# Which engine squares the score tiles of batch 1: GpSimd from the third batch's bursts on only

## The chip, the cores and the metric

One Trainium2 chip, one of its cores. A core has five engines, each with its own queue of instructions that it works through in order: TensorE (PE in the profile; its weight loads are listed apart as PEld), VectorE (DVE), ScalarE (ACT), GpSimd (POOL) and SyncE (SP), which here only issues DMAs. Matmul results go to PSUM, which GpSimd does not read in this kernel; everything else lies in SBUF. The metric is the device time of one execution in microseconds (us); lower is better.

## The reference

Attention with a squared ReLU in place of the softmax, and behind it a feed-forward block whose activation is a squared ReLU too. Cut to what is computed:

```python
# q, k, v: 8 batches, 12 heads, 448 tokens, 64 wide (float32)
scores = scale * np.matmul(q, k.transpose(0, 1, 3, 2))     # scale = 1/8
attn = np.maximum(scores, 0.0) ** 2 / S                    # S = 448
attn_out = np.matmul(attn, v)
x = attn_out.transpose(0, 2, 1, 3).reshape(B * S, H * D)   # 3584 x 768
h = x @ w_in                                               # 768 x 2048
r = np.maximum(h, 0.0)
out = (r * r) @ w_out                                      # 2048 x 768
```

## The kernel before

**Units, rounds, bursts.** Four heads of one batch are a unit `n`; three units make a batch, 24 in all. A unit has seven rounds `t`, each of 64 keys. A round makes one score tile `sp` (eight small matmuls per pair of rounds, L384), squares its positive part into an fp16 tile `at` (`soft`), and later multiplies `at` with v (`av`, L416). The first 23 rounds (batch 0 and two rounds more) are one stream. From there on the rounds go in pairs: burst `i` does rounds `2i` and `2i + 1`, for `i` from 11 to 83 (burst 11 has one round only). Within a burst TensorE first makes the score tiles, then, in the bursts that `avs` names, all seven products of a finished unit (28 matmuls), and then as much of the feed-forward block as `run_some` takes from a queue of pieces of work.

**What fills the bursts.** That queue (`push_dense`) holds for each batch 16 h groups (six matmuls each, L198, with the squared ReLU of h behind them) and the products with w_out. Batch 0 uses plain products (16 matmuls, L236); later batches use a form with fewer products (`o_groups`), which needs sums and differences of blocks of w_out, eight in all, made once by `combine_w2` on GpSimd (L145 to L151) and set between the h groups of batch 0. In bursts 11 to 18 TensorE does two h groups a burst, in bursts 19, 20 and 22 the four plain products.

**Two ways to square a tile.** `relu2` (L179): ScalarE squares the score tile into `at`, and VectorE multiplies `at` with a mask of the positive scores, reading the tile again. `relu2_wide` (L184): ScalarE writes the ReLU in fp32 to a buffer `rel`, of which there are two, and the engine that is named squares it into `at`. Score tiles lie in two PSUM buffers of two banks; the matmul results of all other work rotate through four more banks. The choice is made in `soft` (L390): from burst 12 on the first tile of a burst goes by `relu2`, the second, by `pool=z == 1` (L528), by `relu2_wide` with GpSimd.

**What sets the order.** TensorE and SP run in the order in which the program is written. The order on VectorE, ScalarE and GpSimd is set by the scheduler that builds the program. GpSimd has, beside the squares, the loads of v and of the weights (it issues their DMAs), the casts of k and q to fp16 (L96), the sums of w_out and a copy `rest` (L219). SP has the loads of k and q (L87), their transposes by DMA for units from 6 on (L102), and the stores of the output (L209). `upkeep` names the burst in which each of these is issued.

```python
    NU, TJ = 3, 7                       # units of a batch, rounds of a unit
    def av_burst(n):                    # the burst in which unit n's products run
        return (TJ * (n + 1) - 1) // 2 + 2
```

So the products of units 3, 4, 5 and 6 run in bursts 15, 19, 22 and 26, and `av_burst(2 * NU - 1)`, which the change uses, is 22.

Of the kernel before, what the change touches and what calls it, by code (L numbers as in the profile page):

```python
# [16 lines left out]
def kernel(  # L17
# [20 lines left out]
    NU = 3  # L38
# [131 lines left out]
    def run_some(ns):  # L170
        nonlocal queued, credit
        credit += ns
        while fifo and credit > 0:
            c, fn = fifo.popleft()
            fn()
            queued -= c
            credit -= c

    def relu2(ps, dst, scale):  # L179
        nc.scalar.activation(out=dst, in_=ps, func=AF.Square, scale=scale)  # L180
        nc.vector.scalar_tensor_tensor(  # L181
            out=dst, in0=ps, scalar=0.0, in1=dst, op0=ALU.is_gt, op1=ALU.mult)

    def relu2_wide(ps, dst, scale, eng):  # L184

        r = rel_p.tile([P, 2, S], FP32, name="rel", tag="wide")
        nc.scalar.activation(out=r, in_=ps, func=AF.Relu, scale=scale)  # L187
        eng.tensor_mul(dst, r, r)  # L188
# [149 lines left out]
    def push_dense(b):  # L338

        hs = h_groups(b)  # L340
        if b == 0:
            new = [[g] for c in range(2) for g in plain_groups(chunk(b, c))]
        elif b % 2 == 0:
            new = chain([o_groups(chunk(b, 0), chunk(b, 1))])
        else:
            pr = b // 2
            pairs = [o_groups(chunk(b - 1, 2), chunk(b, 0)), o_groups(chunk(b, 1), chunk(b, 2))]
            if pr % 2 == 1:
                pairs.insert(1, o_groups(rest_chunk(pr - 1), rest_chunk(pr)))
            new = chain(pairs)  # L350
        old = backlog[:QUOTA[b]]
        done = 0
        for i, g in enumerate(hs):
            push([g])
            upto = (i + 1) * len(old) // len(hs)
            for z in old[done:upto]:
                push(z)
            done = upto
            if b == 0 and 4 <= i < 16 and i % 2 == 1:
                push([(0.0, lambda k=(i - 4) // 2: combine_w2(k, nc.gpsimd))])  # L360
        if b % 2 == 1:
            push([(0.0, lambda: rest(b // 2))])
        backlog[:] = backlog[len(old):] + new
        now = QUOTA[b] - len(old)
        for z in backlog[:now]:
            push(z)
        del backlog[:now]
        if b == 0:
            push([(0.0, lambda k=k: combine_w2(k, nc.gpsimd)) for k in (6, 7)])
# [7 lines left out]
    def scores(n, t):  # L377
        qT, kT = qkt[n, "q"], qkt[n, "k"]
        sp = s_p.tile([P, 2, 512], FP32, name="sp", tag="s")
        for e in range(2):  # L380
            for f in range(2):
                c = f ^ e
                r = slice(64 * f, 64 * f + 64)
                nc.tensor.matmul(  # L384
                    sp[64 * c:64 * c + 64, e, 0:S].rearrange("p (t c) -> p t c", t=TJ),
                    lhsT=kT[r, t, 64 * e:64 * e + 64],
                    rhs=qT[r, :, 64 * e:64 * e + 64], start=True, stop=True)
        return sp

    def soft(n, t, sp, pool=False):  # L390
        at = at_p.tile([P, 2, S], FP16, name="at", tag="at")
        if pool:
            relu2_wide(sp[:, :, 0:S], at, SK, nc.gpsimd)
        elif n < NU and t % 2 == 1:
            relu2_wide(sp[:, :, 0:S], at, SK, nc.gpsimd if n == 1 and t == 3 else nc.vector)
        else:
            relu2(sp[:, :, 0:S], at, SK)
        ats[n, t] = at
# [3 lines left out]
    def av(n, t):  # L402

        b, u = divmod(n, NU)
        if n == NU * b and t == 0:
            xts[b] = x_p.tile([P, NM, S], FP16, name="xt", tag="xt")
        vs = vst[n]
        if t == 0:
            avs_open[n] = [mm_p.tile([P, 512], FP32, name="avt", tag="mm") for _ in range(2)]
        ap = avs_open[n]  # L410
        at = ats.pop((n, t))
        for e in range(2):
            for c in range(2):
                f = c ^ e
                r = slice(64 * c, 64 * c + 64)
                nc.tensor.matmul(  # L416
                    ap[f][64 * e:64 * e + 64, 0:S],
                    lhsT=vs[r, e ^ c, t * D:(t + 1) * D],
                    rhs=at[r, e, :],
                    start=(t == 0), stop=(t == TJ - 1), skip_group_check=True)  # L420
        if t < TJ - 1:
            return
        for f in range(2):
            nc.scalar.activation(  # L424
                out=xts[b][:, 2 * u + f, :], in_=ap[f][:, 0:S], func=AF.Copy, scale=CX)

    pool, dve, act = nc.gpsimd.tensor_copy, nc.vector.tensor_copy, nc.scalar.copy
# [9 lines left out]
    def av_burst(n):  # L437
        return (TJ * (n + 1) - 1) // 2 + 2
# [4 lines left out]
    def upkeep(i):  # L443

        for n in range(NU, NUN):
            b, u = divmod(n, NU)
            if i == av_burst(n - 1) and NU + 2 < n + 3 < NUN:
                load_v(n + 3)
            if i == max(TJ * n // 2, STREAM // 2):
                if 5 < n + 3 < NUN:  # L450
                    for w in "kq":
                        load_qk(n + 3, w, nc.sync)
            if i == (TJ * n + 4) // 2:
                if n + 2 < NUN:
                    for w in "kq":
                        cast_qk(n + 2, w, pool)
                if n + 1 < NPE:
                    turn_pe(n + 1, "k", dve)
                    turn_pe(n + 1, "q", act)
                if NPE <= n + 2 < NUN:  # L460
                    for w in "kq":
                        turn_dma(n + 2, w)
# [56 lines left out]
    for i in range(STREAM // 2, NB):  # L519
        g = []  # L520
        for r in range(max(STREAM, 2 * i), 2 * i + 2):
            n, t = divmod(r, TJ)
            g.append((n, t, scores(n, t)))
        if i in avs:
            for t in range(TJ):
                av(avs[i], t)
        for z, a in enumerate(g):
            soft(*a, pool=z == 1)  # L528
        if i in pushes:
            push_dense(pushes[i])  # L530
        upkeep(i)
        nxt = min([j for j in pushes if j > i] or [NB + 2])
        run_some(max(0.0, (queued - KEEP) / (nxt - i)))
# [37 lines left out]
```

## Time and profile before

| | |
|---|---|
| time, median of 2 runs | 424.2 us (424.13 to 424.28) |
| profiled execution, its own time | 422.38 us |
| span of that execution, first to last instruction | 420.6 us |
| mean granted clock of TensorE | 0.963 |
| busy: TensorE, VectorE, ScalarE, GpSimd | 378.7, 259.4, 259.3, 234.9 us |
| squares by GpSimd (L188), number and mean | 73, 1687 ns |
| Relu into `rel` (L187, ScalarE), mean | 922 ns |
| Square into `at` (L180, ScalarE), mean | 915 ns |
| mask of a score tile (L181, VectorE), mean | 1088 ns |

The profiled execution is one run with a hardware profile. Its span leaves out what lies ahead of the first and behind the last instruction, 1.8 us here. A row of a timeline has the start and duration in us, the engine, the line, the operation, what is written and what is read (tile names without buffer numbers), the shape and a count; the bracket at its end holds the time for which the engine had stood idle, and what ended that.

### The profile page before, as it was taken

Reading aid. Unit: us, or ns where it says so; the run is one execution under the profiler, and the core shown is the slowest. Engines: PE = TensorE matmul, PEld = TensorE weight load, DVE = VectorE, ACT = ScalarE, POOL = GpSimd, SP = SyncE. Lnnn points to the kernel's source line nnn. Section 1 sums busy time; section 2 is a strip of 40 time slices with the busy share of each in tenths; the row PEclk is TensorE's granted clock in tenths of the full one; section 3 lists DMA queues with packets and bytes.
Section 4 is the critical chain, followed back from the end, with each engine's and each line's share of the span. In section 5 each row is a group of like instructions: output and inputs, shape, how many; then the busy total and the mean of one; then the engine's idle time right before and its main releaser. Section 6 shows DMA issues by size and latency. Waiting matters only on the chain.

```text
span 420.6 us, 7636 instructions
## 1 busy us (share of the span) xinstructions
PE 378.7 (90%) x3000; PEld 190.2 (45%) x3000; DVE 259.4 (62%) x336; ACT 259.3 (62%) x407; POOL 234.9 (56%) x197
## 2 busy tenths in 40 slices
PE   6847736989999999999999999998998999999995
PEld 2424312444444544444455545544444444555562
DVE  3978521733669367857798655874696566545831
ACT  3888523875876587768856677676765767234111
POOL 6761889989965664865866645736753433200000
PEclk9698955999999999999999999999999999999999
DMA  8999994346715977369247674483633201120243
GB/s 255 295 257 234 238 199 110 67 104 149 218 22 89 216 161 147 68 166 245 60 83 189 169 184 73 145 179 61 170 41 80 59 2 39 37 58 0 51 101 75
DMA packets 67620, 53.58 MB, mean 127 GB/s; under 512 B 36865, under 2 KB 67585, under 8 KB 67585
## 3 DMA queue, kind: packets, MB, share of 16 engines
q1 hardware_dynamic: 55152, 40.84, 38.2%
q0 software_dynamic: 12160, 11.80, 18.4%
q8 instruction: 23, 0.38, 0.4%
q10 hardware_dynamic: 272, 0.46, 0.3%
q14 instruction: 13, 0.10, 0.1%
HBM read 45.61 MB, written 11.01 MB: 135 GB/s over the span
## 4 chain that ended last, share of the span: by engine, by line
PE 70%; DMA 14%; DVE 6%; POOL 3%; issue 3%; ACT 3%; SPq 1%; ACTq 0%; POOLq 0%; DVEq 0%
PE hps L198 31%; PE ops L274 23%; PE sp L384 7%; PE avt L416 6%; DMA w<-in_moe_w_in_dram 6%; DMA w<-in_moe_w_out_dram 5%; DVE comb L253 4%; PE ops L236 3%; DMA early<-in_q_dram 3%; DVE g L181 1%; POOL wt L149 1%; ACT rel L187 1%; ACT g L180 1%; DVE at L181 1%; POOL wt L147 1%
## 5 line engine op out<-in xcount | busy, mean ns | idle before, releaser
L188 POOL TENSOR_TENSOR at<-rel 128x896 f16<-128x896 f32 x73 | 122.8, 1687 | 71.8 <-ACT rel L187 71.6
L198 PE MATMUL hps<-xt,w 128*128 128x448 f16 x768 | 157.4, 356 | 1.0 <-ACT xt L424 0.6
L181 DVE SCALAR_TENSOR_TENSOR g<-hps,g 128x448 f16<-128x448 f32 x128 | 79.5, 624 | 84.5 <-ACT g L180 84.5
L181 DVE SCALAR_TENSOR_TENSOR at<-sp,at 128x896 f16<-128x896 f32 x87 | 94.5, 1088 | 35.7 <-ACT at L180 35.1
L198 PEld LDWEIGHTS <-w 128*128 128x128 f16 x768 | 72.4, 98 | 77.8 <-issue 17.0
L180 ACT ACTIVATE g<-hps 128x448 f16<-128x448 f32 x128 | 69.7, 548 | 54.3 <-PE hps L198 53.8
L180 ACT ACTIVATE at<-sp 128x896 f16<-128x896 f32 x87 | 79.3, 915 | 19.0 <-PE sp L384 18.9
L187 ACT ACTIVATE rel<-sp 128x896 f32<-128x896 f32 x81 | 74.7, 922 | 21.4 <-POOL at L188 17.1
L384 PE MATMUL sp<-qT,kT 64*64 64x448 f16 x672 | 53.6, 375 | 23.2 <-ACT rel L187 13.0
L274 PEld LDWEIGHTS <-comb 128*128 128x128 f16 x416 | 39.1, 98 | 34.8 <-DVE comb L253 5.2
L280 ACT ACTIVATE part<-ops 128x384 f32<-128x384 f32 x52 | 25.7, 494 | 47.0 <-PE ops L274 46.1
L416 PE MATMUL avt<-at,vs 64*64 64x448 f16 x672 | 43.7, 369 | 8.2 <-POOL at L188 7.1
L285 DVE SCALAR_TENSOR_TENSOR osb<-ops,part 128x384 f32<-128x384 f32 x52 | 28.4, 551 | 27.9 <-ACT part L280 17.7
L384 PEld LDWEIGHTS <-kT 64*64 64x64 f16 x672 | 16.5, 107 | 55.6 <-issue 53.0
L274 PE MATMUL ops<-wt,comb 128*128 128x384 f16 x208 | 36.5, 327 | 2.8 <-DVE comb L253 2.8
L274 PE MATMUL ops<-w,comb 128*128 128x384 f16 x208 | 36.8, 326 | 0.0
L96 POOL CAST ks<-kf 128x896 f16<-128x896 f32 x21 | 20.3, 969 | 29.1 <-DMA kf<-in_k_dram 26.4
L121 POOL DMA_DIRECT2D vs<-in_v_dram x48 | 30.0, 632 | 9.2 <-PE avt L416 6.0
L274 PEld LDWEIGHTS <-g 128*128 128x128 f16 x264 | 25.0, 98 | 19.5 <-issue 3.4
L416 PEld LDWEIGHTS <-vs 64*64 64x64 f16 x672 | 22.3, 112 | 20.9 <-issue 10.1
L274 PE MATMUL ops<-w,g 128*128 128x384 f16 x176 | 30.9, 326 | 0.0
L219 POOL COPY rest<-g 128x1024 f16<-128x1024 f16 x8 | 10.4, 1294 | 29.8 <-DVE g L181 29.8
(43 smaller groups left out, 216.8 us busy)
## 6 DMA issues: line engine op xcount, KB each, us to landing
out_dram<-osb SPq DMA_DIRECT2D x112, 96.0 KB, 2.2
kf<-in_k_dram SPq DMA_DIRECT2D x22, 448.0 KB, 4.1
qf<-in_q_dram SPq DMA_DIRECT2D x21, 448.0 KB, 4.8
vs<-in_v_dram POOLq DMA_DIRECT2D x48, 112.0 KB, 3.3
w<-in_moe_w_in_dram POOLq DMA_DIRECT2D x4, 768.0 KB, 20.3
w<-in_moe_w_out_dram POOLq DMA_DIRECT2D x4, 768.0 KB, 19.3
early<-in_k_dram SPq DMA_DIRECT2D x2, 448.0 KB, 7.5
early<-in_q_dram SPq DMA_DIRECT2D x2, 448.0 KB, 9.1
```

The lines of the kernel that those rows point to most:

```text
L96: op(t.rearrange("p t (f d) -> p f t d", f=2), src.rearrange("p f (t d) -> p f t d", d=D))
L121: nc.gpsimd.dma_start(out=t[64 * r:64 * r + 64], in_=src[:, u, hs])
L180: nc.scalar.activation(out=dst, in_=ps, func=AF.Square, scale=scale)
L181: nc.vector.scalar_tensor_tensor(out=dst, in0=ps, scalar=0.0, in1=dst, op0=ALU.is_gt, op1=ALU.mult)
L187: nc.scalar.activation(out=r, in_=ps, func=AF.Relu, scale=scale)
L188: eng.tensor_mul(dst, r, r)
L198: nc.tensor.matmul(hps[:, 0:S], lhsT=w1[f // 4][:, m, (f % 4) * P:(f % 4 + 1) * P], rhs=xt[:, m, :], start=(m == 0), stop=(m == NM - 1))
L274: nc.tensor.matmul(st[bank][:, 0:HALF], lhsT=st[a][:, j, :], rhs=w(j), start=(first and j == 0), stop=(j == NH - 1), skip_group_check=True)
L280: nc.scalar.activation(out=st[name], in_=st[bank][:, 0:HALF], func=AF.Copy, scale=CO)
L285: nc.vector.scalar_tensor_tensor(out=osb, in0=st[bank][:, 0:HALF], scalar=sign * CO, in1=st[name], op0=ALU.mult, op1=ALU.add)
L384: nc.tensor.matmul(sp[64 * c:64 * c + 64, e, 0:S].rearrange("p (t c) -> p t c", t=TJ), lhsT=kT[r, t, 64 * e:64 * e + 64], rhs=qT[r, :, 64 ...
L416: nc.tensor.matmul(ap[f][64 * e:64 * e + 64, 0:S], lhsT=vs[r, e ^ c, t * D:(t + 1) * D], rhs=at[r, e, :], start=(t == 0), stop=(t == TJ - ...
```

## The change

Of the second tile of a burst, those of bursts 12 to 22 now go by `relu2`, ScalarE and VectorE alone; from burst 23 on GpSimd squares them as before.

```diff
         for z, a in enumerate(g):
-            soft(*a, pool=z == 1)
+            soft(*a, pool=z == 1 and i > av_burst(2 * NU - 1))
         if i in pushes:
             push_dense(pushes[i])
```

GpSimd's queue from the first sums of w_out on (`wt_107`, `wt_108` and `wt_109` are the results of the first three steps, `w_0` to `w_3` the blocks of w_out), before against now:

```order
 L145 TENSOR_TENSOR wt_107<-w_1_104 128x1536
-L188 TENSOR_TENSOR at<-rel 128x896
 L96 CAST ks<-kf 128x2x7x64
 L96 CAST qs<-qf 128x2x7x64
 L147 TENSOR_TENSOR wt_108<-w_2_105,wt_107 128x1536
 L147 TENSOR_TENSOR wt_108<-w_3_106,wt_107 128x1536
-L188 TENSOR_TENSOR at<-rel 128x896
 L149 TENSOR_TENSOR wt_109<-wt_108,w_2_105 128x1536
 L149 TENSOR_TENSOR wt_109<-wt_108,w_3_106 128x1536
-L188 TENSOR_TENSOR at<-rel 128x896 x2
 L121 DMA vs<-in_v_dram 64x2x448 x2
```

The sums now follow one another with only the two casts of unit 6 between them; behind them come the v load and the casts of units 7 and 8. Seven more squares go further down, up to the last step of the sums (L151); the order of the other work is the same.

VectorE's queue in bursts 12 to 14, before:

```order
L181 SCALAR_TENSOR_TENSOR at<-sp,at 128x896
L181 SCALAR_TENSOR_TENSOR g<-hps,g 128x448 x2
L181 SCALAR_TENSOR_TENSOR at<-sp,at 128x896
L181 SCALAR_TENSOR_TENSOR g<-hps,g 128x448 x2
L181 SCALAR_TENSOR_TENSOR at<-sp,at 128x896
```

and now:

```order
L181 SCALAR_TENSOR_TENSOR at<-sp,at 128x896 x2
L181 SCALAR_TENSOR_TENSOR g<-hps,g 128x448 x2
L181 SCALAR_TENSOR_TENSOR at<-sp,at 128x896 x2
L181 SCALAR_TENSOR_TENSOR g<-hps,g 128x448 x2
L181 SCALAR_TENSOR_TENSOR at<-sp,at 128x896 x2
```

Each burst has a second mask of a score tile ahead of the masks of its two h groups; on ScalarE a Square stands where the Relu stood.

SP's queue is the same before and now. From the transposes of unit 6 on it reads:

```order
L102 DMA_TRANSPOSE kT<-ks 128x7x128
L102 DMA_TRANSPOSE qT<-qs 128x7x128
L87 DMA kf<-in_k_dram 128x2x448
L87 DMA qf<-in_q_dram 128x2x448
L102 DMA_TRANSPOSE kT<-ks 128x7x128
L102 DMA_TRANSPOSE qT<-qs 128x7x128
L209 DMA out_dram<-osb 64x384 x4
L87 DMA kf<-in_k_dram 128x2x448
L87 DMA qf<-in_q_dram 128x2x448
```

The second pair of transposes is that of unit 7, the loads ahead of it are those of unit 8, and those behind the four stores (the first two plain products) are those of unit 9. Nothing moved here; the rows show what stands in front of what.

## The prediction

> **What bounds the kernel now.** I read the page first, then the chain that ended last, then the timeline of each engine between 40 and 110 us, where the moved tiles lie. From the page, the span in 40 slices of 10.5 us:
>
> ```profile
> PE   6847736989999999999999999998998999999995
> POOL 6761889989965664865866645736753433200000
> PEclk9698955999999999999999999999999999999999
> ```
>
> From the eighth slice on TensorE is nearly always busy at full clock, so a gain there would need fewer matmuls, and the change removes none. The loss sits in slices five to seven, where TensorE is busy 3, 6 and 9 tenths and its clock falls to half, while GpSimd (POOL) is at 8, 9 and 9 tenths. Those slices are bursts 14 to 17. TensorE there, in order of time (start, duration, group, and in brackets the idle time before it and what ended it):
>
> ```profile
> 44.53 2.44 PE L198 MATMUL hps<-xt,w 128*128 128x448 f16 x12
> 46.91 0.57 PE L384 MATMUL sp<-qT,kT 64*64 64x448 f16 x8
> 47.41 2.44 PE L198 MATMUL hps<-xt,w 128*128 128x448 f16 x12
> 56.66 0.96 PE L384 MATMUL sp<-qT,kT 64*64 64x448 f16 x8 [6.81 <-ACT rel L187]
> ...
> 66.93 0.59 PE L416 MATMUL avt<-at,vs 64*64 64x448 f16 x4 [7.07 <-POOL at L188]
> 67.45 4.66 PE L198 MATMUL hps<-xt,w 128*128 128x448 f16 x12
> 72.04 0.70 PE L384 MATMUL sp<-qT,kT 64*64 64x448 f16 x8
> 81.97 0.57 PE L384 MATMUL sp<-qT,kT 64*64 64x448 f16 x8
> 82.37 1.49 PE L416 MATMUL avt<-at,vs 64*64 64x448 f16 x28
> 83.80 2.77 PE L236 MATMUL ops<-w,g 128*128 128x384 f16 x16
> ```
>
> Two waits stand out, 6.81 us ahead of burst 15 and 7.07 us inside it. GpSimd and ScalarE (ACT) show why:
>
> ```profile
> 46.30 3.09 POOL L145 TENSOR_TENSOR wt<-w 128x1536 f16<-128x1536 f16 x1 [0.48 <-DMA w<-in_moe_w_out_dram]
> 50.94 3.08 POOL L145 TENSOR_TENSOR wt<-w 128x1536 f16<-128x1536 f16 x1 [1.54 <-DMA w<-in_moe_w_out_dram]
> 53.98 1.68 POOL L188 TENSOR_TENSOR at<-rel 128x896 f16<-128x896 f32 x1
> 55.69 0.92 ACT L187 ACTIVATE rel<-sp 128x896 f32<-128x896 f32 x1 [7.33 <-POOL at L188]
> 57.57 3.09 POOL L147 TENSOR_TENSOR wt<-w,wt 128x1536 f16<-128x1536 f16 x1 [0.16 <-DMA w<-in_moe_w_out_dram]
> 62.16 3.08 POOL L147 TENSOR_TENSOR wt<-w,wt 128x1536 f16<-128x1536 f16 x1 [1.50 <-DMA w<-in_moe_w_out_dram]
> 65.20 1.68 POOL L188 TENSOR_TENSOR at<-rel 128x896 f16<-128x896 f32 x1
> 66.83 6.13 POOL L149 TENSOR_TENSOR wt<-wt,w 128x1536 f16<-128x1536 f16 x2
> 76.19 1.26 POOL L121 DMA_DIRECT2D vs<-in_v_dram  x2
> 77.42 0.96 POOL L96 CAST ks<-kf 128x896 f16<-128x896 f32 x1
> 78.29 0.96 POOL L96 CAST qs<-qf 128x896 f16<-128x896 f32 x1
> ```
>
> GpSimd works in order. The square at 53.98 stands behind two sums of w_out (L145) that wait for their blocks to land; only when it ends is one of the two `rel` buffers free, ScalarE's next Relu runs at 55.69, the score tile is released, and TensorE goes on at 56.66. The square at 65.20 stands in the same way behind L147, whose last block lands at 62.16, and the fourth product of unit 3 needs that tile.
>
> **The change, term by term.** Eleven tiles (the second of bursts 12 to 22) leave GpSimd. ScalarE still runs one pass over each, Square in place of Relu. VectorE (DVE) gains a mask pass for each, and a score tile is now released by VectorE and not by ScalarE. No DMA is added and the order of TensorE and SP is unchanged.
>
> *Removed: the two waits and the half clock.* The waits are 6.81 + 7.07 = 13.9 us. Burst 15 runs from 56.66 to 72.04, 15.4 us; less its 7.07 it is 8.3. At full clock the same work is a score pair 0.50 (46.91 to 47.41), an `av` 1.33 (81.97 to 83.80 less 0.50) and two h groups 2.38 (44.53 to 46.91): 4.2. So the half clock costs 4.1. Together 18.0 us. The clock is not a separate hope: it falls after the waits, and the new schedule has no wait above 1.2 us.
>
> *Added: VectorE in bursts 13 to 19.* Durations:
>
> ```profile
> 35.21 2.09 DVE L181 SCALAR_TENSOR_TENSOR at<-sp,at 128x896 f16<-128x896 f32 x2 [0.30 <-ACT at L180]
> 58.32 1.09 DVE L181 SCALAR_TENSOR_TENSOR at<-sp,at 128x896 f16<-128x896 f32 x1
> 79.33 1.16 DVE L181 SCALAR_TENSOR_TENSOR g<-hps,g 128x448 f16<-128x448 f32 x2 [0.16 <-ACT g L180]
> ```
>
> A burst with two h groups then costs VectorE 2.09 + 1.16 = 3.25 us, against 0.50 + 2.38 = 2.88 on TensorE: VectorE becomes the slower by 0.37 a burst. It owes this in five bursts (14, 15, 17, 18, 19); the `av` of burst 15 and the transposes of burst 16 keep TensorE busy while VectorE catches up. 5 x 0.37 = 1.9 us of waits ahead of the score pairs. ScalarE has the same pass count as before, so I cost its swap at nothing; the cover is that its passes are of equal length (0.91 and 0.92 in the next rows).
>
> *Added: bursts 21 and 22, which have little or no filler work between their score pairs:*
>
> ```profile
> 90.21 0.91 ACT L180 ACTIVATE at<-sp 128x896 f16<-128x896 f32 x1
> 91.00 0.92 ACT L187 ACTIVATE rel<-sp 128x896 f32<-128x896 f32 x1
> 91.15 1.09 DVE L181 SCALAR_TENSOR_TENSOR at<-sp,at 128x896 f16<-128x896 f32 x1 [2.12 <-ACT at L180]
> 91.98 0.70 PE L384 MATMUL sp<-qT,kT 64*64 64x448 f16 x8 [1.69 <-ACT rel L187]
> ```
>
> Burst 22 starts at 91.98, right behind the Relu (91.92). In its place its second tile waits for a second mask, which follows the first at 92.24 and ends at 93.3; that half would have started near 92.2. So 1.1 us, and by the same reckoning 0.2 at burst 21: 1.3 us.
>
> *Moved up: GpSimd's own chain, then the next wait.* With nothing between the sums, GpSimd is bound by the landing of w_out at 62.16, which I hold fixed. L147 to 65.2, L149 to 71.4, the v load 1.2, then the casts of unit 7 at 72.6 and 73.5 (0.87 apart), those of unit 8, `rest` and a v load, free at 78.4. SP:
>
> ```profile
> 78.41 1.23 SPq L102 DMA_TRANSPOSE kT<-ks  x1
> 79.74 1.25 SPq L102 DMA_TRANSPOSE qT<-qs  x1
> 87.13 4.31 SPq L209 DMA_DIRECT2D out_dram<-osb  x4
> 91.49 0.58 SPq L87 DMA_DIRECT2D kf<-in_k_dram  x1
> ```
>
> The transposes of unit 7 stood 7 us ahead of the first stores. Now TensorE ends its first plain group near 70 while they go out only at 73.6 to 76.2, so four stores queue behind them on SP, and behind those the loads of unit 9: out at about 78.5 instead of a full 15 us ahead of 91.49, which would be 76.5. Landing takes 4.1 (k) and 4.8 (q), by the last two rows below; the casts of unit 9 on GpSimd then end near 84.6, a v load at 85.9, and the last sums (L151, 6.16) run to 92.0, then the squares of bursts 23 and 24.
>
> ```profile
> 98.84 6.16 POOL L151 TENSOR_TENSOR w<-w,w 128x1536 f16<-128x1536 f16 x2
> 104.94 3.32 POOL L188 TENSOR_TENSOR at<-rel 128x896 f16<-128x896 f32 x2
> 106.99 0.92 ACT L187 ACTIVATE rel<-sp 128x896 f32<-128x896 f32 x1
> kf<-in_k_dram SPq DMA_DIRECT2D x22, 448.0 KB, 4.1
> qf<-in_q_dram SPq DMA_DIRECT2D x21, 448.0 KB, 4.8
> ```
>
> The Relu of burst 25 (106.99 before, about 91.9 after 15 us of gain) needs the `rel` buffer that the square of burst 23 frees at 93.7. ScalarE stands 1.8 us; the masks of three h groups are late and the `av` of burst 26 waits for a PSUM bank. TensorE loses about 1.0. No row of before shows this wait. Below it is nothing (GpSimd's chain a little quicker); above it is the full 1.8 plus as much as w_out lands later, since other loads come forward beside it (third rival). I take 1.0, nearest to the ScalarE row.
>
> *Costed at nothing.* The plain groups need all of w_out (landed 62.16) and start near 67, so 5 us cover the landing. The transposed tiles of unit 7 are needed by burst 24, near 86, and leave SP by 76.2. From burst 27 on every engine's order is that of before, so the rest shifts whole.
>
> Sum: 18.0 - 1.9 - 1.3 - 1.0 = 13.8 us. The profiled execution took 422.38 us (span 420.6), so it would be 408.6 (span 406.8). The median of the runs shown, 424.2, is 1.8 above that execution; I forecast against the median: 410.4 us.
>
> [...] VectorE's mask passes now run beside GpSimd's sums. The row at 58.32 is such a pass inside the L147 of 57.57 to 60.66, and took 1.09, as elsewhere, so I lengthen none of them. [...]
>
> **Rivals.**
> *The whole gain comes.* The casts of unit 9 are not late, or VectorE's debt hides behind TensorE's other work: only 1.3 to 2 us are lost, 424.2 - 16.5 = 407.7 us. For it: the GpSimd term is the least certain one. Against it: 3.25 is more than 2.88 in any order.
> *Slower: VectorE and GpSimd exclude each other.* Six sums between 46.30 and 72.96 are 18.5 us in which no mask would run. VectorE's last mask of burst 18 would come 18.5 later, the gain of 13.8 turns into a loss of 4.7, and the time is 428.9. It decides from about three quarters (13.8 of 18.5) blocked. Against it: the 58.32 row.
> *GpSimd's chain gets longer.* w_out lands 2 to 4 us later because the transposes of unit 6 and the loads of unit 8 come forward, by the 1.6 us of the square at 53.98, into the DMA that is still bringing w_out; the wait at bursts 25 and 26 grows by as much: 412.5 to 414.5, say 413.5 us.
> *VectorE and ScalarE do not overlap.* If in each burst from 13 to 20 the two squares and the h masks ran ahead of the second mask one after another, a burst would last 0.50 + 0.80 + 0.91 + 1.09 + 1.16 = 4.46, 1.58 more than TensorE's 2.88; 8 x 1.58 = 12.6 instead of 1.9 leaves a gain of 3.1: 421.1 us.
> That the tiles don't move is not open: the built order has eleven squares less on GpSimd.
>
> **How the numbers follow.** Forecast 0.48, whole gain 0.20, longer chain 0.20, no overlap 0.07, exclusion 0.03, other losses 0.02. The range takes the first three cases: from all of 18.0 kept (406.2) to the longer chain's end (414.5); 0.12 lie beyond it. Two per cent, about what a measurement of this kernel can tell from no change, is 8.5 us, 415.7. Faster by over that: 0.48 + 0.20 + 0.20 = 0.88; within it no overlap and exclusion, 0.10; slower by over 2% 0.02.
>
> **What would show it.** No idle time over 1.5 us on TensorE between 40 and 84 us, and the clock at 9 in slices five to seven. Score pairs of bursts 14 to 19 that wait for VectorE, some 0.4 us each. The first plain group near 67 instead of 83.80. ScalarE's Relu of burst 25 waiting for GpSimd's square, behind L151. I am wrong if masks beside L145 to L149 last longer than 1.09, if the plain groups wait for w_out, or if a new wait of over 2 us stands between bursts 20 and 27.

## The result, and the profile after

The changed kernel takes 411.94 us (median of 2 runs, 411.39 to 412.48) against 424.2 us before: a ratio of 0.9711, with a 95% interval of 0.9655 to 0.9766. Faster, by 12.3 us where 13.8 was forecast, and inside the range of 406.2 to 414.5. Six more runs, reported below, have a median of 411.09. The profiled execution has a span of 410.6 us (time 412.48). Its page, in 40 slices of the span as before:

```profile
PE   6757999798999999999999999999979999999995
POOL 5851778669666568467846664754743335101000
PEclk9885999999999999999999999999998999999998
```

The prediction counts the slices from zero; counted from one, its three are slices six to eight, bursts 14 to 19 before. There TensorE reads 9, 9 and 7, where it read 3, 6 and 9, and its clock reads 9 throughout, where it read 5, 5 and 9. The 7 holds a wait ahead of burst 22. Slice four got worse (the clock at 5, where it was at 8).

Busy time of each engine between the score pair of burst 12 and that of burst 27, before and after (the first number is the stretch, the next the busy time in it, then the same for weight loads, VectorE, ScalarE and GpSimd, and the granted clock; the last two numbers, the share of the DMA engines and GB/s, are not used):

```profile
40.00:105.00 65.00, 48.65 (x387) 23.94 (x387) 26.27 (x34) 36.29 (x56) 59.50 (x42) 0.84 0.74 146
40.04:113.86 73.82, 57.47 (x463) 28.00 (x462) 31.99 (x42) 43.18 (x67) 67.34 (x48) 0.86 0.77 160
```

```profile
42.64:102.40 59.76, 54.28 (x464) 27.15 (x463) 41.08 (x51) 43.42 (x67) 47.31 (x35) 1.00 0.89 189
```

The first row is the kernel before from 40 to 105 us, where GpSimd was busy for 59.5 of 65. The other two are the same work before and after: 73.82 us became 59.76. TensorE's idle time in it fell from 16.4 to 5.5 us and its busy time by 3.2 (clock 0.86, now 1.00), while VectorE has 9.1 us more to do and GpSimd 20.0 less.

What is left of TensorE's waits there:

```profile
49.97 0.38 PE L384 MATMUL sp<-qT,kT 64*64 64x448 f16 x4 [0.36 <-DVE at L181]
64.33 0.38 PE L384 MATMUL sp<-qT,kT 64*64 64x448 f16 x4 [0.33 <-DVE at L181]
69.03 2.77 PE L236 MATMUL ops<-w,g 128*128 128x384 f16 x16
77.53 0.38 PE L384 MATMUL sp<-qT,kT 64*64 64x448 f16 x4 [1.83 <-DVE at L181]
78.52 0.38 PE L384 MATMUL sp<-qT,kT 64*64 64x448 f16 x4 [0.61 <-DVE at L181]
78.71 1.52 PE L416 MATMUL avt<-at,vs 64*64 64x448 f16 x28
87.73 0.70 PE L384 MATMUL sp<-qT,kT 64*64 64x448 f16 x8 [0.45 <-ACT rel L187]
97.48 0.57 PE L384 MATMUL sp<-qT,kT 64*64 64x448 f16 x8 [1.52 <-ACT rel L187]
98.58 1.51 PE L416 MATMUL avt<-at,vs 64*64 64x448 f16 x27 [0.37 <-DVE g L181]
102.40 0.57 PE L384 MATMUL sp<-qT,kT 64*64 64x448 f16 x8
```

The waits of 6.81 and 7.07 are gone. Bursts 14 and 18 wait a third of a microsecond for a mask, burst 22 waits 2.4 for two of them, and burst 26 waits for a Relu. Behind that Relu stands GpSimd's chain, seen on GpSimd, ScalarE and SP:

```profile
62.72 3.09 POOL L147 TENSOR_TENSOR wt<-w,wt 128x1536 f16<-128x1536 f16 x1 [1.49 <-DMA w<-in_moe_w_out_dram]
65.77 6.14 POOL L149 TENSOR_TENSOR wt<-wt,w 128x1536 f16<-128x1536 f16 x2
84.04 0.93 POOL L96 CAST ks<-kf 128x896 f16<-128x896 f32 x1 [5.30 <-issue]
86.62 0.93 POOL L96 CAST qs<-qf 128x896 f16<-128x896 f32 x1 [1.65 <-DMA qf<-in_q_dram]
88.68 6.17 POOL L151 TENSOR_TENSOR w<-w,w 128x1536 f16<-128x1536 f16 x2
94.81 3.31 POOL L188 TENSOR_TENSOR at<-rel 128x896 f16<-128x896 f32 x2
96.52 0.92 ACT L187 ACTIVATE rel<-sp 128x896 f32<-128x896 f32 x1 [3.18 <-POOL at L188]
75.38 1.24 SPq L102 DMA_TRANSPOSE qT<-qs  x1
76.72 2.48 SPq L209 DMA_DIRECT2D out_dram<-osb  x4
79.25 0.59 SPq L87 DMA_DIRECT2D kf<-in_k_dram  x1
79.89 0.53 SPq L87 DMA_DIRECT2D qf<-in_q_dram  x1
```

The transposes of unit 7 leave SP by 76.6, four stores follow, the loads of unit 9 go out at 79.25 and 79.89 and have landed only for 84.04 and 86.62 on GpSimd, where L151 follows until 94.8 and then the square that the Relu needs. It waits 3.18 us.

The sum, stretch by stretch, needs three more rows of the kernel before:

```profile
40.04 0.90 PE L384 MATMUL sp<-qT,kT 64*64 64x448 f16 x8
92.48 1.52 PE L416 MATMUL avt<-at,vs 64*64 64x448 f16 x28
113.86 0.57 PE L384 MATMUL sp<-qT,kT 64*64 64x448 f16 x8
```

| stretch | before | after | gain | forecast |
|---|---|---|---|---|
| burst 12 to the first plain product | 43.76 | 26.39 | 17.4 | 18.0 - 1.9 = 16.1 |
| from there to the products of unit 5 (burst 22) | 8.68 | 9.68 | -1.0 | -1.3 |
| from there to burst 27 | 21.38 | 23.69 | -2.3 | -1.0 |
| burst 12 to burst 27 | 73.82 | 59.76 | 14.1 | 13.8 |
| start to burst 12 | 40.04 | 42.64 | -2.6 | 0 |
| burst 27 to the end of the span | 306.7 | 308.2 | -1.5 | 0 |

The two profiled spans differ by 10.0 us and not by 14.1, because of the last two rows, which lie outside the bursts that the change edits. The first experiment is on them.

### The profile page after: what moved, and what is told of

The parts are those of the page before. It is cut to its first block, busy times and chain, and to the rows that moved or that the text cites. A ratio compares the mean times of both kernels' runs of the same rounds, so it can differ in the third digit from the quotient of the medians.

```text
span 410.6 us, 7636 instructions
## 1 busy us (share of the span) xinstructions
PE 380.4 (93%) x3000; PEld 190.4 (46%) x3000; DVE 269.2 (66%) x347; ACT 259.6 (63%) x407; POOL 216.6 (53%) x186
## 4 chain that ended last, share of the span: by engine, by line
PE 74%; DVE 9%; ACT 7%; DMA 3%; issue 3%; POOL 2%; SPq 1%; ACTq 0%; DVEq 0%; POOLq 0%
PE hps L198 33%; PE ops L274 24%; PE sp L384 8%; PE avt L416 7%; DVE comb L253 4%; DVE at L181 3%; ACT at L180 2%; ACT rel L187 2%; DMA qf<-in_q_dram 2%; POOL w L151 2%; DVE g L181 1%; PE ops L236 1%; ACT g L180 1%; DMA kf<-in_k_dram 1%; PE tps L110 1%
## 5 line engine op out<-in xcount | busy, mean ns | idle before, releaser
L188 POOL TENSOR_TENSOR at<-rel 128x896 f16<-128x896 f32 x62 | 104.2, 1685 | 72.2 <-ACT rel L187 72.1
L181 DVE SCALAR_TENSOR_TENSOR at<-sp,at 128x896 f16<-128x896 f32 x98 | 105.4, 1088 | 32.9 <-ACT at L180 32.6
L180 ACT ACTIVATE at<-sp 128x896 f16<-128x896 f32 x98 | 88.3, 916 | 19.7 <-PE sp L384 19.6
L187 ACT ACTIVATE rel<-sp 128x896 f32<-128x896 f32 x70 | 64.7, 924 | 6.8 <-PE sp L384 3.6
```

Of the source, the lines that this page charges most:

```text
L181: nc.vector.scalar_tensor_tensor(out=dst, in0=ps, scalar=0.0, in1=dst, op0=ALU.is_gt, op1=ALU.mult)
```

## The experiments

There are nine experiments. The stretch from burst 12 to burst 27, counted from the score pairs on TensorE in the one profile of each, stands beside the time. When burst 12 starts is left out of it, but a half clock within it is not.

**1. The changed kernel again.** No edit.

> The changed kernel once more, unaltered. Theory: from burst 12 to burst 27 the time is 59.8 us again, since every wait there is set by the order of the queues; what differs from execution to execution is how TensorE's half clock falls on the same waits ahead of burst 12 and at bursts 74 to 76. So burst 12 starts somewhere between 40.0 and 42.7 us and the stretch from burst 27 to the end lasts 306.7 to 308.3. Rival: the change itself delays burst 12 and the end, and both come out as in the first profile (42.6 and 308.2). Time 411 to 412.5 us by both.

Measured: 411.09 us (6 runs, 409.28 to 411.79), ratio 0.971 (0.9683 to 0.9737). Bursts 12 to 27 took 59.67 us, as expected, but not every wait was the same again. The waits of 1.83 and 0.61 us at burst 22 came back, and here the clock fell to half behind them:

```profile
78.45 2.55 PE L416 MATMUL avt<-at,vs 64*64 64x448 f16 x28
80.93 5.98 PE L236 MATMUL ops<-w,g 128*128 128x384 f16 x32
```

The products took 1.52 in the first profile; burst 22 lasted 9.58 us instead of 7.94. TensorE therefore came later to burst 26 while GpSimd's chain did not (L151 starts at 88.37, 88.68 in the first profile), and no wait was left ahead of that burst: bursts 25 and 26 took 8.84 instead of 10.52. The later loss hides in the earlier one.

Burst 12 started at 42.42, and the stretch from burst 75 to burst 83 took 37.23 us as in the kernel before, against 38.88 in the first profile of the changed kernel. The end is thus a matter of the execution. The start is too, as the other runs show: in the profiles of the experiments up to the eighth, whose queues are alike up to burst 12, it starts at 42.39, 41.16, 42.14, 42.64, 42.82, 42.83 and 40.83. The 42.83 is experiment 7, the kernel before with an edit at burst 15, so a late start does not need the change. The only profile of the kernel before, at 40.04, was the quickest of all at this point. In 45 later runs that kernel took 421.7 to 427.1 us, with medians of 423.19, 422.98 and 422.93 in three groups, so the 424.2 of two runs, from which the forecast was counted, was some 1.1 us high. What differs at the start is TensorE's clock: the same two h groups of burst 11, before (granted clock 1.00) and after (0.50):

```profile
37.66 2.44 PE L198 MATMUL hps<-xt,w 128*128 128x448 f16 x12
```

```profile
38.05 4.66 PE L198 MATMUL hps<-xt,w 128*128 128x448 f16 x12
```

**2. The squares of bursts 23 and 24 on VectorE too.**

```diff
-            soft(*a, pool=z == 1 and i > av_burst(2 * NU - 1))
+            soft(*a, pool=z == 1 and i > 24)
```

> The squares of bursts 23 and 24 go to VectorE too (13 tiles moved). Theory (GpSimd's last sums, L151, hold the two rel buffers and with them the Relu of burst 25): that Relu finds both buffers free, the wait of 1.52 us ahead of burst 26 and the 0.37 in its products go, about 1.9 us, and burst 24 loses some 0.5 because its score tiles now wait for a mask: 410.5 us, 1.2 to 1.9 faster than the changed kernel. Rival (the loss at burst 26 has another cause, such as the masks of the h groups): no gain, 412 us.

Measured: 409.44 us (6 runs), ratio 0.9686 (0.9658 to 0.9715), 1.65 below the first experiment, which ran on the same chip. Bursts 12 to 27 took 58.40. The clock stayed full behind burst 22 (which lasted 7.94 us), as in the first profile of the changed kernel, and the wait of 1.52 ahead of burst 26 that stands there is gone; burst 24 waits 0.77 and 0.62 for masks instead. That is what was expected if GpSimd's chain is the cause.

**3. The loads of unit 9 ahead of the stores on SP.**

```diff
-            if i == max(TJ * n // 2, STREAM // 2):
+            if i == (19 if n == 6 else max(TJ * n // 2, STREAM // 2)):
```

> The loads of unit 9 are issued in burst 19, on SP ahead of the four stores of the first plain products instead of behind them. Theory (SP's order makes the loads late, these the casts of unit 9 on GpSimd, these L151): loads out near 76.7 instead of 79.25, L151 ends near 92.3 instead of 94.85, the Relu of burst 25 waits 0.7 instead of 3.18, TensorE gains 1.5 to 2.3 us: 410 us. Rival (L151 is bound by the plain products that read its target, not by the casts ahead of it): L151 stays and the time too, 412 us.

Measured: 408.97 us (6 runs), ratio 0.9669 (0.964 to 0.9699); bursts 12 to 27 took 59.05. L151 and the Relu of burst 25:

```profile
86.10 6.19 POOL L151 TENSOR_TENSOR w<-w,w 128x1536 f16<-128x1536 f16 x2
93.95 0.92 ACT L187 ACTIVATE rel<-sp 128x896 f32<-128x896 f32 x1 [0.50 <-POOL at L188]
```

L151 starts 2.3 us sooner than in the first experiment and ends at 92.3, and the Relu waits 0.5. SP's order is what made the chain late. The median is 2.1 lower; the stretch of this profile, which has the half clock behind burst 22 like that of the first experiment, is only 0.6 shorter.

**4. L151 on VectorE.**

```diff
-            push([(0.0, lambda k=k: combine_w2(k, nc.gpsimd)) for k in (6, 7)])
+            push([(0.0, lambda k=k: combine_w2(k, nc.vector)) for k in (6, 7)])
```

> The last two sums of w_out (L151) are made by VectorE instead of GpSimd. Theory: GpSimd reaches the squares of bursts 23 and 24 by 91.5, the Relu of burst 25 does not wait, and the 1.9 us at burst 26 go; VectorE, idle for 5.9 us ahead of burst 23, has room for two sums of 1 to 3 us each: 410 us. Rival (the sums on VectorE, beside GpSimd's casts, delay the masks of burst 23 and take the gain back): 412 us or more.

Measured: 408.33 us (6 runs), ratio 0.9656 (0.9625 to 0.9688), 2.8 below the first experiment; bursts 12 to 27 took 59.04, in the slowest of the six runs (411.07). The Relu of burst 25 does not wait, and VectorE needs 2.56 us for the two sums where GpSimd needs 6.17.

What experiments 2, 3 and 4 show together, with each burst counted from its first score matmul to that of the next:

| profile | burst 22 | bursts 25 and 26 | bursts 12 to 27 |
|---|---|---|---|
| kernel before | 7.26 | 8.21 | 73.82 |
| changed kernel | 7.94 | 10.52 | 59.76 |
| 1, the same again | 9.58 | 8.84 | 59.67 |
| 2, squares of 23 and 24 on VectorE | 7.94 | 8.21 | 58.40 |
| 3, loads ahead of stores | 9.58 | 8.22 | 59.05 |
| 4, L151 on VectorE | 9.58 | 8.21 | 59.04 |

They cut the chain at three different places, and each time bursts 25 and 26 are as short as before: the cause of that loss is settled. Its size depends on the clock behind burst 22: 2.3 us where it stays full, 0.6 where it falls to half and TensorE comes late anyway. The three medians are 1.6 to 2.8 us below that of the first experiment, but the intervals of the ratios overlap with its own, so the times do not fix the size.

**5. Four tiles moved instead of eleven.**

```diff
-            soft(*a, pool=z == 1 and i > av_burst(2 * NU - 1))
+            soft(*a, pool=z == 1 and i > 15)
```

> Only the second tiles of bursts 12 to 15 go to VectorE (four instead of eleven). Theory (what costs is any square that stands in GpSimd's queue behind the sums, and the sums end near 72 us whatever else is done): the square of burst 16 cannot start before the sums and the casts of unit 7 are done, near 74.8, so the Relu of burst 18 waits from 64 to 76.5; TensorE stands about 10 us ahead of burst 19 and loses some clock behind it; bursts 12 to 27 take 68 to 72 us instead of 59.7, and the time is 419 to 423 us, most of the gain gone. Rival (the two waits of the profile before were the whole cost, and both belong to the squares of bursts 12 and 13): no wait, and the masks of bursts 16 to 22 saved too: 409 to 410 us.

Measured: 420.92 us (9 runs), ratio 0.9937 (0.9916 to 0.9958); bursts 12 to 27 took 68.06. GpSimd, ScalarE and TensorE:

```profile
65.61 6.12 POOL L149 TENSOR_TENSOR wt<-wt,w 128x1536 f16<-128x1536 f16 x2
74.65 1.70 POOL L188 TENSOR_TENSOR at<-rel 128x896 f16<-128x896 f32 x1
76.38 0.92 ACT L187 ACTIVATE rel<-sp 128x896 f32<-128x896 f32 x1 [11.32 <-POOL at L188]
77.35 0.96 PE L384 MATMUL sp<-qT,kT 64*64 64x448 f16 x8 [10.80 <-ACT rel L187]
```

The square of burst 16 starts at 74.65 and the Relu of burst 18 at 76.38, both within 0.2 of what was expected. The two waits of 6.81 and 7.07 were only the first that the profile before showed: taking away the tiles in front moves the wait to the next square, and most of the gain is lost.

**6. GpSimd squares from burst 19 on.**

```diff
-            soft(*a, pool=z == 1 and i > av_burst(2 * NU - 1))
+            soft(*a, pool=z == 1 and i > 18)
```

> The second tiles of bursts 12 to 18 go to VectorE, GpSimd squares from burst 19 on. Theory: GpSimd reaches the square of burst 19 near 77.6 and that of burst 20 near 80.5, behind the casts of units 7 and 8; the Relu of burst 21 and the products of unit 5 in burst 22 wait for them, 2 to 4 us, and the casts of unit 9 and L151 move back: bursts 12 to 27 take 62 to 64 us, time 413.5 to 415.5 us. Rival (GpSimd is free in time once the sums are done, and VectorE's masks at bursts 19 to 22 are the larger cost): 1 us faster than the changed kernel, 410 us.

Measured: 412.94 us (4 runs), ratio 0.9753 (0.9721 to 0.9785); bursts 12 to 27 took 60.43. The direction of the stretch is as expected, the size is not. Burst 22 waits 4.20 us for a Relu, a little more than expected, but there is no wait ahead of burst 26 any more: TensorE now comes there so late that GpSimd's chain is done. The two losses do not add; the later hides in the earlier, as in the first experiment. The interval of the ratio overlaps with that of the first experiment, so that this version is slower at all rests on the wait and the stretch.

**7. The kernel before, with TensorE kept busy in its two waits.**

```diff
+    def fill(count):
+        ps = mm_p.tile([P, 512], FP32, name="fill", tag="mm")
+        for _ in range(count):
+            nc.tensor.matmul(ps, lhsT=ident, rhs=w1[0][:, 0, :], start=True, stop=True)
...
         g = []
+        if i == 15:
+            fill(26)
...
             for t in range(TJ):
+                if i == 15 and t == TJ - 1:
+                    fill(28)
                 av(avs[i], t)
```

> The kernel before, with 26 matmuls of no use in the wait ahead of burst 15 and 28 ahead of the fourth product in it (their result is read by nobody). Theory (the half clock is a cost beside the waits, 4.1 us in the sum): the clock stays full, so what follows the second wait, 66.93 to 72.04 before, takes 2.6 us instead of 5.1; the 1.6 us ahead of that wait are hidden by it. About 2.5 us faster than the kernel before: 420.7. Rival (the clock is low for another reason than the waits): the same 5.1 us and the same time, 423.2, or more where the added matmuls reach past the wait.

Measured: 424.23 us (12 runs), ratio 1.0023 (0.9999 to 1.0047): no gain; bursts 12 to 27 took 72.59. (The product that waits is the seventh and last of unit 3, not the fourth; the edit stands at it, at `t == TJ - 1`.) TensorE:

```profile
66.51 0.38 PE L421 MATMUL avt<-at,vs 64*64 64x448 f16 x4 [0.79 <-POOL at L188]
66.83 2.44 PE L198 MATMUL hps<-xt,w 128*128 128x448 f16 x12
75.21 0.38 PE L384 MATMUL sp<-qT,kT 64*64 64x448 f16 x4 [2.27 <-ACT rel L187]
76.32 4.12 PE L198 MATMUL hps<-xt,w 128*128 128x448 f16 x12
```

The clock stayed full: the two h groups behind the second wait took 2.44 us where they had taken 4.66. But two bursts later TensorE stands waiting for a Relu, which waits for the squares behind L149, and the clock falls there instead (4.12 us for two h groups). Burst 16 starts at 69.20 where it started at 72.04, but burst 18 at 80.38 where it started at 79.09. So the half clock was no cost of its own in the kernel before; TensorE at full clock only comes sooner to the next square that GpSimd has not made. The added matmuls also take two turns of the four PSUM banks that rotate, and the stretch from burst 27 to burst 75 was 3.1 us longer in this profile (206.6 against 203.5). That this comes from the rotation is argued and was not tried, and this profile is of the slowest of the twelve runs (426.87); it may be why the time is a little above that of the kernel before and not equal to it.

**8. The better version: experiment 4, and GpSimd squares again in bursts 21 and 22.**

```diff
-            push([(0.0, lambda k=k: combine_w2(k, nc.gpsimd)) for k in (6, 7)])
+            push([(0.0, lambda k=k: combine_w2(k, nc.vector)) for k in (6, 7)])
...
-            soft(*a, pool=z == 1 and i > av_burst(2 * NU - 1))
+            soft(*a, pool=z == 1 and i > 20)
```

> The changed kernel with the sums of L151 on VectorE (as in the run e4_dve151) and with GpSimd squaring the second tiles of bursts 21 and 22 again, where it is idle from 78 us on. Theory: the Relu releases the score tile of burst 21 one us sooner than the mask, so burst 22 starts 2.3 us behind burst 21 as in the kernel before, the waits of 1.83 and 0.61 us go, and no clock is lost in the plain products behind them; the squares, started at 78.4, are done by 82: 1.0 to 1.6 us faster than e4_dve151, near 407 us. Rival: the two squares stand ahead of the casts of unit 9 and some wait further down takes the gain: 408.3.

Measured: 407.47 us (6 runs, 405.4 to 409.04), ratio 0.9623 (0.9596 to 0.965), the fastest here. Its stretch from burst 12 to burst 27:

```profile
40.83:97.57 56.74, 53.93 (x463) 26.93 (x462) 42.24 (x53) 43.33 (x67) 44.70 (x35) 1.00 0.97 194
```

56.74 us with 2.8 us of idle time on TensorE. Burst 22 waits 1.51 for a Relu, about as in the kernel before, and nothing else is over half a microsecond. In time it is 0.9 below experiment 4, and the intervals of the two ratios overlap, so the time does not show the second half of the edit. The stretch is 2.3 shorter than the 59.04 of experiment 4, but 1.6 of that is the half clock behind burst 22 in that profile, which two of the five profiles with the same waits escaped. What the edit is shown to give is burst 21 at 2.27 instead of 2.58 and burst 22 at 7.26 instead of 7.94, the value at full clock: 1.0 us, of which burst 12 lost 0.3 to the clock in this profile. That the shorter wait also keeps the clock up is likely, but not shown: the clock stayed full behind it (burst 22 at 7.26 us) in all five profiles that have it.

**9. The kernel before, with the sums on VectorE and the squares left on GpSimd.**

```diff
-                push([(0.0, lambda k=(i - 4) // 2: combine_w2(k, nc.gpsimd))])
+                push([(0.0, lambda k=(i - 4) // 2: combine_w2(k, nc.vector))])
...
-            push([(0.0, lambda k=k: combine_w2(k, nc.gpsimd)) for k in (6, 7)])
+            push([(0.0, lambda k=k: combine_w2(k, nc.vector)) for k in (6, 7)])
```

> The kernel before, with all eight sums of w_out on VectorE and every square left on GpSimd. In its built order the masks of bursts 12 and 13 stand on VectorE behind L145 and L147, as the squares stood on GpSimd. Theory (the loss is score tiles held by work that stands behind a wait for w_out to land, whichever engine has the sums): the mask of burst 13 runs only after the last block has landed near 62.2 and its sum is made, so TensorE stands ahead of burst 14 or 15 until some 65 us; bursts 12 to 27 take 71 to 76 us, the time is 420 to 425 us, no gain over the kernel before although VectorE needs 1.3 us for a sum where GpSimd needs 3.1. Rival (the loss is GpSimd's load, 59.5 of 65 us busy, and its slow sums): with 24.9 us of sums taken off it there is no wait, and the time is 408 to 410 us.

Measured: 424.23 us (10 runs), ratio 1.0021 (0.9999 to 1.0043); bursts 12 to 27 took 71.76. VectorE, and the longest waits of TensorE:

```profile
57.90 2.14 DVE L147 TENSOR_TENSOR wt<-w,wt 128x1536 f16<-128x1536 f16 x1 [3.01 <-DMA w<-in_moe_w_out_dram]
62.00 0.96 DVE L147 TENSOR_TENSOR wt<-w,wt 128x1536 f16<-128x1536 f16 x1 [0.90 <-DMA w<-in_moe_w_out_dram]
62.88 1.08 DVE L181 SCALAR_TENSOR_TENSOR at<-sp,at 128x896 f16<-128x896 f32 x1
48.64 0.59 PE L384 MATMUL sp<-qT,kT 64*64 64x448 f16 x4 [5.78 <-DVE at L181]
64.02 0.59 PE L384 MATMUL sp<-qT,kT 64*64 64x448 f16 x4 [5.55 <-DVE at L181]
```

GpSimd is idle for 3.2 to 6.5 us between its squares there, the sums are up to three times as quick (0.94 us against 3.09), and nothing is gained. A mask stands behind a sum that waits for the last block of w_out at 62.0, and TensorE stands behind the mask. What cost the time was not GpSimd's speed or load but work that frees score tiles, queued behind a wait for a DMA.

## Why the prediction was right

*Where the time was lost, and by what.* Right. Squares behind the sums, the sums behind the landing of w_out; experiments 5 and 9 show it from two sides, and the landing itself stayed (62.16 before, 62.72 after), as held fixed in the prediction. The last product of unit 3, the seventh, is the one that waited; the prediction calls it the fourth.

*The term of 18.0 us.* Right in size: bursts 14 and 15 lasted 9.75 and 15.38 us, and without a wait and at full clock they last 2.88 (burst 13 before) and 4.20 (burst 15 in experiment 9), 18.05 less. Another 0.8 came from bursts 12, 16 and 17, which the prediction did not count; the 0.3 of burst 12 comes and goes with the clock. The term is wrong in its parts. The prediction listed 13.9 of waits and 4.1 of half clock as two costs that are removed. Experiment 7 took away the half clock behind the second wait alone and gained nothing (424.23 us), since GpSimd's next squares were not ready sooner. The 4.1 us were to be had only with the waits.

*VectorE in bursts 13 to 19, 1.9 us.* Near in size: 1.5. Against the same bursts at full clock with the squares on GpSimd (2.88, 4.20, 2.88 and 4.53 in experiment 9 and the kernel before), bursts 14 and 18 last some 0.5 longer and 15 and 19 some 0.2; only 0.7 of it shows as idle time in the rows. The count was wrong: five equal debts were taken, and burst 17 pays next to nothing.

*Bursts 21 and 22, 1.3 us.* 1.0, by the mechanism described: the second mask releases the tile. One sign failed: I said no idle time over 1.5 us before 84 us, and the wait ahead of burst 22 is 1.83 (with 0.61 for its second half). It stands at the place where the kernel before had one of 1.69.

*GpSimd's chain and burst 26, 1.0 us.* The step that had no row of before was right in every link (transposes ahead of stores, loads late, L151 late, Relu waiting), and mis-sized: 2.3 in the first profile, 0.6 in the second, where TensorE came later. In the first, the load of q of unit 9 needed until 86.62, 6.6 us behind its issue instead of the 4.8 taken, and w_out landed 0.6 later; the Relu waits 3.18 and not 1.8. Experiments 2, 3 and 4 each cut one link, and bursts 25 and 26 then lose nothing.

*VectorE beside GpSimd, and the second rival.* Two masks beside L147 took 2.09 us together:

```profile
62.19 2.09 DVE L181 SCALAR_TENSOR_TENSOR at<-sp,at 128x896 f16<-128x896 f32 x2 [0.18 <-ACT at L180]
```

as elsewhere (mean 1086 to 1088 ns in the groups by line). No run here shows a mask of a score tile held up by GpSimd, so the exclusion did not come. Sums on VectorE did last longer beside GpSimd's work, in experiments 4 and 9; see the last section.

*The other rivals.* The longer chain came in part, inside the forecast. No overlap did not come: bursts 13 to 19 with two h groups last 2.9 to 3.4 us, not 4.46.

*The time itself.* 410.4 against 411.94 in 2 runs and 411.09 in 6, in part by luck. The stretch that the change touches gained 14.1 against 13.8, but that is a sum of errors that cancel: 0.8 not counted, 0.4 and 0.3 costed too high, 1.3 too low. The medians differ by 12 and not 13.8, and the time came out close because the 424.2 from which it was counted was some 1.1 us high. The spans of the two profiles differ by 10.0: of the 4.1 us beside the stretch, 2.2 are the half clock at burst 11 and 1.6 that at bursts 75 to 83.

## What to carry to other kernels

When a wait is found behind an in-order queue, look at the whole queue before costing its removal: the next instruction of the same kind may stand behind the same obstacle (experiment 5, a wait of 10.80 us), and moving the obstacle to another engine moves the wait with it (experiment 9, waits of 5.78 and 5.55). A slow clock behind a stall was no second gain here, with the engine that caused the stall still behind (experiment 7, 424.23 us). And a part that runs earlier meets the queues that did not: SP's order between transposes and stores, harmless for as long as TensorE was late, became the next wait (3.18 us of a Relu).

## What was not expected of the hardware

**Behind the same wait the clock falls in some executions and not in others.** At bursts 74 to 76 the queues and the waits are the same in all kernels here (0.60 and 2.08 us ahead of two score pairs, behind VectorE's sums). In the eleven profiles the stretch from burst 75 to burst 83 lasts 37.23 or 37.24 us seven times, and 38.87 or 38.88 four times. In the slow ones the products behind the wait run at half clock (2.36 to 2.88 us instead of 1.52); the same wait of 2.08 us in the kernel before and after:

```profile
319.98 0.38 PE L384 MATMUL sp<-qT,kT 64*64 64x448 f16 x4 [2.08 <-DVE at L181]
320.16 1.52 PE L416 MATMUL avt<-at,vs 64*64 64x448 f16 x28
```

```profile
308.35 0.38 PE L384 MATMUL sp<-qT,kT 64*64 64x448 f16 x4 [2.08 <-DVE at L181]
308.54 2.44 PE L416 MATMUL avt<-at,vs 64*64 64x448 f16 x28
```

With up to 2.8 us at burst 12 (40.04 to 42.83), this can set two executions of one kernel further apart than most of the experiments above do; the 45 later runs of the kernel before lie between 421.7 and 427.1. Burst 22 is a third such place: behind its waits of 1.83 and 0.61 us the clock fell in three of the five profiles that have them, 9.58 us against 7.94. In the first profile of the changed kernel the granted clock is 0.50 from 308.99 to 312.39 and 1.00 on both sides, 3.4 us; half of that is lost, about the 1.64 between the two lengths. What decides whether the clock falls behind such a wait, and what ends the stretch of half clock, no run here shows.

**Of a sum of w_out on VectorE and GpSimd's work beside it, one or both last longer; a mask does not.** In experiment 9 a sum on VectorE takes 0.96 us alone (46.62) and 2.14 in the row at 57.90, beside a square of GpSimd that runs from 57.55 to 59.23; the sum at 51.36 takes 1.47, and the square of GpSimd beside it, which starts at 51.99, 2.38 instead of 1.68. In experiment 4 the two sums of L151 take 2.56 together, and a cast of GpSimd beside them 1.61 instead of 0.93:

```profile
84.77 2.56 DVE L151 TENSOR_TENSOR w<-w,w 128x1536 f16<-128x1536 f16 x2 [4.32 <-POOL ks L96]
84.92 1.61 POOL L96 CAST qs<-qf 128x896 f16<-128x896 f32 x1 [0.17 <-DMA qf<-in_q_dram]
```

The masks of score tiles show none of it: the one at 53.28 in experiment 9, beside that same square, takes 1.07, and in the changed kernel the two at 62.19 beside L147 take 2.09. What sets the sums apart from the masks was not shown.
